# Two adjacent PSUM banks in one instruction: joined exponentials and joined row maxima in a two-attention kernel

## The chip, the cores and the metric

The kernel runs on one core of one Trainium2 chip. Its time is the device time of one execution in microseconds (us), and the figure that counts is the median of several runs. Five engines with queues of their own take part: TensorE (PE in the profile, with PEld for its weight loads), VectorE (DVE), ScalarE (ACT), GpSimd (POOL) and SyncE (SP, which here issues transfers). A matmul writes its result into PSUM, a memory of eight banks; one bank holds 512 float32 values in each of 128 partitions. ACT and DVE read the banks and so make them free again.

## The reference

Two attentions over the same 2048 tokens of width 576, mixed by a gate. A has a key and a value for each of its 32 heads; B has one key and one value that all its 32 heads share. A head has 18 columns.

```
x = A_x                                            # 1 x 2048 x 576
g = sigmoid((x * gate_w).sum(-1, keepdims=True))
# A: q, k, v of each head from x @ wqkv
p = softmax(einsum("bhqd,bhkd->bhqk", q, k) * 18 ** -0.5)
a = merge(einsum("bhqk,bhkd->bhqd", p, v)) @ wo
# B: q of each head from x @ wq; k = x @ wk, v = x @ wv for all heads
p = softmax(einsum("bhqd,bkd->bhqk", q, k) * 18 ** -0.5)
b = merge(einsum("bhqk,bkd->bhqd", p, v)) @ wo
out = g * a + (1 - g) * b
```

The B weights wq and wk are drawn eight times larger than the others, so its scores are large and each row's maximum has to be subtracted before the exponential.

## The kernel before

**The heads.** 64 heads are worked through one after the other, the 32 of B first. For one head there are 2048 x 2048 scores. They are needed twice: once to find each query row's maximum, and once, with the maximum already subtracted, for the exponential.

**A step.** A head has 16 steps, one for each tile of 128 rows. T counts steps from the first head to the last (1024 in all), and the loop at the end of the program advances by two steps, so that a head is eight *pairs* of steps. In a pair, with the tiles called A and B, there is:

- *Scores* (`step_scores`, L553): four matmuls a tile (`sA0` to `sB3`), each of 128 keys against 512 queries into one PSUM bank `ps`; after each an exponential on ACT (L560) from the bank into `pt` in SBUF. Eight of each in a pair.
- *Maxima* (`step_max`, L515): matmuls of 128 queries against 512 keys into a bank `pm` (`mA2` and the like), for a head that is 22 steps (`LEAD`) ahead, and a row maximum on DVE (L524) of each. Of the first tile of a pair, two of the four pieces are taken together: a matmul `x` with the difference of two pieces of keys goes into a `ps` bank, ACT writes its positive part to `xb` (L518), and DVE adds `xb` to the other piece and takes the maximum in one instruction (L521). So a pair has six plain maxima, one of L521, eight score matmuls, one `x`, and nine ACT instructions.
- *PV* (`step_pv`, L566): the exponentials times the values, accumulated over the whole head into one bank `acc`. Four matmuls for four groups of 512 queries stand side by side in four column groups of the array. A PV step can be done whole (512 columns) or in two halves (256). Scores and PV are one pair apart: the pair T does the PV of steps T-2 and T-1.

Score matmuls use partitions 0 to 55 and maxima partitions 64 to 117, so a score and a maximum that follow each other can run in the array at the same time; two scores, or two maxima, cannot.

**The order.** Nothing is scheduled automatically. Strings of tokens give the order within a pair: `s` and `m` as above, `x`, then `P`/`Q` for a whole PV step and `p`/`f`/`h`/`H` for halves, and `U` for a unit of the output projection. `PLAIN` and its variants (`END`, `AFTER`, `BEFORE_ROWS`, `ROWS`) are used where no unit is due. `UNIT` and `UNIT_END` are for 32 pairs between T = 522 and T = 848, where the projection of the B heads is spread out (heads with one unit and heads with two). `UNIT2` is for 25 pairs between T = 944 and T = 998, nearly every pair there. A unit (`out_proj`, L695) is 12 matmuls of 288 columns into a `pm` bank and one ACT or DVE instruction that adds it to `oacc`. The last 11 pairs have orders of their own (`ALONE`, `LAST`).

**Other work around it.** At the end of a head DVE copies `acc` to `oe` (`head_out`, L588), and three pairs before a head begins its maxima are reduced and transposed (`max_rows`, L530 and L532). SP carries the queries and keys of the next heads and the heads' outputs. About every seventh head DVE also computes reciprocals of row sums (L617).

**PSUM.** Three pools: `ps_s` with four banks (`ps`: scores, `x`), `ps_m` with three (`pm`: maxima, units) and `ps_o` with one (`acc`). A matmul waits until the bank that comes round in its pool has been read. `pt` has 12 slots of 512 values.

## Time and profile before

| | |
|---|---|
| median of 3 runs | 2668.65 us (2668.41 to 2670.15) |
| span of the profiled execution | 2669.7 us (no other time of that execution is recorded) |
| granted TensorE clock in it | 0.999 |
| PE busy | 2652.4 us (99%) |
| DVE busy | 2421.4 us (91%) |
| ACT busy | 2393.3 us (90%) |
| POOL busy | 283.8 us (11%) |

Stages, by the copies of `acc` to `oe` that end each head and by the first score matmul at 275.4 us: projections and set-up until about 275 us; 32 heads and a half without units until about 1437 us, of 35.5 to 36.1 us each; 22 heads with one or two units until about 2250 us, of 36.0 to 39.0 us; 5 heads without units until about 2393 us; then 7 units a head, 46.4 to 46.7 us each, and the last head and the end of the projection.

The profile's busy share of ACT and DVE counts an instruction from its start to its end; two that follow each other overlap a little, so the mean duration of one is longer than the distance between two. PE's matmuls are pipelined, so its busy share says little; its work is better read from the distances between starts, or from the chain of waits, where a piece ends when the next begins.

### The profile page before, as it was taken

What the parts mean: (1) busy time and instruction counts of PE and PEld (TensorE: products, weight loads), DVE (VectorE), ACT (ScalarE), POOL (GpSimd) and SP (SyncE); (2) the same over time, 40 slices, a digit from 0 to 9 for tenths busy, and PEclk for the clock granted to TensorE, in tenths of its full rate; (3) what the DMA queues carried; (4) which work ended last, traced back from release to release, by engine and by line L of the source; (5) the groups of instructions that cost most, each with busy time, mean ns of one, the idle gap of its engine ahead of it and who ended that gap; (6) DMA issues with size and microseconds to landing.
All of it is one profiled execution on the core that took longest, in us unless ns stands there. A gap on an engine that the chain in (4) does not pass through costs nothing.

```text
span 2669.7 us, 58607 instructions
## 1 busy us (share of the span) xinstructions
PE 2652.4 (99%) x22278; PEld 898.0 (34%) x22278; DVE 2421.4 (91%) x4588; ACT 2393.3 (90%) x4814; POOL 283.8 (11%) x526
## 2 busy tenths in 40 slices
PE   9999999999999999999999999999999999999998
PEld 7778322222222222222222222222222222223444
DVE  8447999999999999999999999999999999998873
ACT  4341899999999999999999999999999999998875
POOL 4740000001001100100110002000200011001000
PEclk9999999999999999999999999999999999999999
DMA  7332000011001100210132112112121212122312
GB/s 202 125 112 76 23 20 20 20 37 40 28 17 46 44 20 18 54 33 20 36 77 82 43 53 85 43 55 59 58 67 51 55 54 61 40 70 86 90 36 95
DMA packets 127304, 150.15 MB, mean 56 GB/s; under 512 B 55456, under 2 KB 94744, under 8 KB 125933
## 3 DMA queue, kind: packets, MB, share of 16 engines
q1 hardware_dynamic: 112593, 119.38, 15.7%
q0 software_dynamic: 8096, 19.30, 2.1%
q10 hardware_dynamic: 6332, 7.71, 0.8%
q8 instruction: 175, 2.87, 0.4%
q14 instruction: 108, 0.88, 0.1%
HBM read 90.80 MB, written 46.45 MB: 51 GB/s over the span
## 4 chain that ended last, share of the span: by engine, by line
PE 93%; DVE 5%; ACT 1%; DMA 1%; issue 1%; SPq 0%; ACTq 0%; DVEq 0%
PE acc L566 38%; PE ps L553 26%; PE pm L515 13%; PE pm L695 4%; PE ps L515 4%; PE ps L248 3%; PE pm L248 3%; DVE mx L524 2%; PE ps L297 2%; DVE junk L521 0%; ACT pt L560 0%; DVE norm_a L190 0%; DVE pl L262 0%; DMA R<-r_d 0%; DVE oacc L772 0%
## 5 line engine op out<-in xcount | busy, mean ns | idle before, releaser
L560 ACT ACTIVATE pt<-ps 128x512 f32<-128x512 f32 x4074 | 2105.6, 651 | 63.1 <-PE ps L553 51.5
L524 DVE TENSOR_REDUCE mx<-pm 128x1 f32<-128x512 f32 x3072 | 1914.1, 682 | 68.0 <-PE pm L515 34.0
L553 PE MATMUL ps<-qs,ksb 56*128 56x512 f16 x2688 | 807.3, 380 | 0.0
L515 PE MATMUL pm<-ksb,qs 54*128 54x512 f16 x2341 | 762.5, 380 | 1.1 <-DVE mx L524 0.6
L566 PE MATMUL acc<-pt,vb 128*19 128x256 f32 (+1 forms) x6144 | 592.4, 457 | 0.0
L566 PE MATMUL acc<-pt,vg 128*19 128x256 f32 (+1 forms) x5496 | 561.7, 480 | 0.3
L515 PEld LDWEIGHTS <-qs 54*128 54x128 f16 x4096 | 293.1, 94 | 516.1 <-issue 455.4
L553 PE MATMUL ps<-qs,ksa 56*128 56x512 f16 x1386 | 407.5, 380 | 0.3
L515 PE MATMUL pm<-ksa,qs 54*128 54x512 f16 x1232 | 399.8, 380 | 1.6 <-DVE mx L524 1.1
L553 PEld LDWEIGHTS <-ksb 56*128 56x128 f16 x2688 | 202.4, 93 | 487.5 <-issue 446.3
L521 DVE CUSTOM_DVE_ANT_0 junk<-pm,xb 128x512 bf16<-128x512 f32 x501 | 341.0, 681 | 9.4 <-PE pm L515 9.0
L518 ACT ACTIVATE xb<-ps 128x512 f32<-128x512 f32 x501 | 319.6, 638 | 7.7 <-PE ps L553 7.3
L534 POOL TENSOR_SCALAR mt<-mt 128x32 f32<-128x32 f32 x64 | 18.6, 290 | 1626.4 <-DVE mt L532 1626.4
L553 PEld LDWEIGHTS <-ksa 56*128 56x128 f16 x1408 | 100.6, 94 | 233.1 <-issue 213.5
L566 PEld LDWEIGHTS acc<-pt,vb 128*19 128x19 f32 x6144 | 104.3, 97 | 216.1 <-issue 208.6
L566 PEld LDWEIGHTS acc<-pt,vg 128*19 128x19 f32 x5496 | 93.2, 97 | 213.1 <-issue 209.7
L515 PE MATMUL ps<-kdb,qs 54*128 54x512 f16 x373 | 140.5, 377 | 0.1
L300 ACT ACTIVATE vst<-ps 128x288 f32<-128x288 f32 x32 | 13.2, 412 | 60.6 <-PE ps L297 60.6
L256 ACT ACTIVATE ph<-ps,tv 128x512 f16<-128x512 f32 x29 | 19.8, 687 | 49.3 <-PE ps L248 34.3
L256 ACT ACTIVATE ph<-pm,tv 128x512 f16<-128x512 f32 x27 | 18.3, 687 | 48.0 <-PE pm L248 29.4
L703 DVE TENSOR_TENSOR oacc<-pm,oacc 128x288 f32<-128x288 f32 x32 | 14.6, 457 | 46.0 <-PE pm L695 45.9
L262 DVE SCALAR_TENSOR_TENSOR pl<-pm,tv,ph 128x512 f16<-128x512 f32 x27 | 20.0, 748 | 37.5 <-ACT ph L256 24.5
(167 smaller groups left out, 1544.6 us busy)
## 6 DMA issues: line engine op xcount, KB each, us to landing
qs<-qkh SPq DMA_DIRECT2D x244, 72.0 KB
qs<-qkl SPq DMA_DIRECT2D x122, 72.0 KB
onh<-oh SPq DMA_DIRECT2D x32, 256.0 KB
onl<-ol SPq DMA_DIRECT2D x32, 256.0 KB
oih<-onh SPq DMA_DIRECT2D x16, 512.0 KB
oil<-onl SPq DMA_DIRECT2D x16, 512.0 KB
ot<-oe SPq DMA_DIRECT2D x220, 36.0 KB
qkh<-ph POOLq DMA_DIRECT2D x56, 128.0 KB, 2.1
```

The costliest lines, as they stand in the source:

```text
L248: nc.tensor.matmul(fp[:, a0:b0], w[a][:kr, k, :], X[b][:kr, k, s0 + a0:s0 + b0], start=(n == 0), stop=(n == len(PROJ) - 1), skip_group_che ...
L256: nc.scalar.activation(h, fp, AF.Copy, scale=t)
L262: nc.vector.scalar_tensor_tensor(l, fp, t, h, op0=OP.mult, op1=OP.subtract)
L297: nc.tensor.matmul(fp[:, 0:288], X[b][:kr, k, st_ * P:(st_ + 1) * P], w[a][:kr, k, :], start=(n == 0), stop=(n == len(PROJ) - 1))
L515: nc.tensor.matmul(pm, qs[u % 3][b:b + 54, i * P:(i + 1) * P], k, start=True, stop=True)
L518: nc.scalar.activation(MX["x", u, i], pm, AF.Relu)
L521: nc.vector.tensor_tensor_reduce(junk, pm, MX.pop(("x", u, i)), 1.0, -3e38, op0=OP.add, op1=OP.max, accum_out=MX[u][:, i, c:c + 1])
L524: nc.vector.tensor_reduce(MX[u][:, i, c:c + 1], pm, axis=AX.X, op=OP.max)
L553: nc.tensor.matmul(ps, kst(u)[b:b + 56, i * P:(i + 1) * P], qs[u % 3][b:b + 56, x * 512:(x + 1) * 512], start=True, stop=True)
L560: nc.scalar.activation(pt, ps, AF.Exp, scale=SCALE / LIFT ** 2)
L566: nc.tensor.matmul(acc[32 * j:32 * j + 19, a:b], v_of(u, i), PT[u, i, j][:, a:b], start=(i == 0 and a == 0), stop=(i == 15), skip_group_ch ...
L695: nc.tensor.matmul(fp[:, 0:288], o[b][:r, t, s2 * P:(s2 + 1) * P], w[a][:r, t, 288 * hf:288 * hf + 288], start=(n == 0), stop=(n == 3 * nt ...
```

## The change

PSUM becomes one tile `bk` of eight banks: 0 to 3 for scores and `x`, 4 to 6 for maxima and units, 7 for `acc`. Two counters give the next bank of each ring (`next_s`, `next_m`) and are set to zero at the start of each head. `pt` becomes one tile of 16 slots, with a counter of its own.

Where the new order has an `S`, its score and the one before lie in adjacent banks, and one ACT instruction takes both banks, 1024 values, into two adjacent slots of `pt`. Where it has an `N`, its maximum and the one before are taken by one DVE instruction, which writes two columns, if their banks are adjacent (a unit shifts the ring, so that in heads with units some are not joined). A head without units has 11 joined exponentials and 7 joined maxima. Over the kernel there are 688 joined exponentials and 373 joined maxima.

The orders of all pairs up to T = 1000 are new: eight strings for the eight pairs of a head, with `c` for the piece that L521 reads, and `p0h`, `p0f`, `p1h`, `p1f` for half or whole PV steps of the earlier and the later tile. The same eight strings with `U` at the end are used where a unit is due.

```diff
-    ps_s = ctx.enter_context(tc.tile_pool(name="ps_s", bufs=4, space=PSUM))
-    ps_m = ctx.enter_context(tc.tile_pool(name="ps_m", bufs=3, space=PSUM))
-    ps_o = ctx.enter_context(tc.tile_pool(name="ps_o", bufs=1, space=PSUM))
+    ps = ctx.enter_context(tc.tile_pool(name="ps", bufs=1, space=PSUM))
...
-    acc = ps_o.tile([P, 512], F32, name="acc")
+    bk = ps.tile([P, 8, 512], F32, name="bk")
+    acc = bk[:, 7, :]
+    RING = {"s": 0, "m": 0}
+
+    def next_s():
+        RING["s"] += 1
+        return (RING["s"] - 1) % 4
+
+    def next_m():
+        RING["m"] += 1
+        return 4 + (RING["m"] - 1) % 3
...
-        L["pt"] = ctx.enter_context(tc.tile_pool(name="ppool", bufs=12, side="left"))
+        L["pt"] = ctx.enter_context(tc.tile_pool(name="ppool", bufs=1, side="left")).tile([P, 16, 512], F32, name="pt")
...
+        elif join == "first":
+            MX["j"] = (n, 4 * i + c)
+        elif join == "second":
+            n0, c0 = MX.pop("j")
+            assert (n, 4 * i + c) == (n0 + 1, c0 + 1)
+            flat = MX[u].rearrange("p i c -> p (i c)")
+            nc.vector.tensor_reduce(flat[:, c0:c0 + 2], bk[:, n0:n0 + 2, :], axis=AX.X, op=OP.max)
...
+    def exps(q):
+
+        if len(q) == 2 and q[0][0] + 1 != q[1][0]:
+            exps(q[:1])
+            exps(q[1:])
+            return
+        n, k = q[0][0], len(q)
+        t = next_pt(k)
+        nc.scalar.activation(L["pt"][:, t[0]:t[0] + k, :], bk[:, n:n + k, :], AF.Exp, scale=SCALE / LIFT ** 2)
...
-    PLAIN = "mB1 mB3 sA0 sA1 mA3 sA2 P mB2 sA3 x sB0 mA2 sB1 mB0 h sB2 mA0 H sB3"
-    UNIT2 = "sA0 mA3 sA1 mB0 sA2 P sA3 mB1 sB0 mB2 sB1 x U mA2 sB2 mA0 sB3 Q mB3"
...
+    PLAIN = ("s c s m S s N p0h m s p0h m s s m x s m p1f",
+             "s s m S N s m p0f x m s c S p1h s m s m p1h",
+             "m s s m p0h x s m s s m p0h s m N S p1h c s p1h",
+             "s m s m x m s p0f s c m s S N s p1h m S p1h",
+             "s c m s m s x p0h m s m s p0h s m S N s p1f",
+             "s m s m S m s p0f m s m x s s N p1h c s p1h",
+             "m s x m s S N p0h c s p0h m s s m s s m p1f",
+             "s c m x s m S p0h s m p0h s m m s S s m p1f")
...
+        if T % 16 == 0:
+            RING["s"] = RING["m"] = 0
...
+            if op in "sS":
+                k = ns.index(n)
+                step_scores(*divmod(T + k // 4, 16), k % 4, hold=k < 7 and ops[ns[k + 1]] == "S")
```

Three places in the order of the instructions follow. In the rows, `ps`, `pm` and `acc` are the banks before, `bk` any bank of the changed kernel; `pt` are exponentials, `xb` the positive part, `mx` the maxima of a head, `qs`, `ksa`, `ksb`, `kda` queries and keys, and a number behind a name tells one copy of a tile from another.

On ACT, over some pairs of a head without units, before:

```order
L560 ACTIVATE pt<-ps 128x512 x8
L518 ACTIVATE xb<-ps 128x512
L560 ACTIVATE pt<-ps 128x512 x10
L518 ACTIVATE xb<-ps 128x512
L560 ACTIVATE pt<-ps 128x512 x7
```

and changed:

```order
L577 ACTIVATE pt<-bk 128x512 x3
L530 ACTIVATE xb<-bk 128x512
L577 ACTIVATE pt<-bk 128x512 x2
L577 ACTIVATE pt<-bk 128x1024
L577 ACTIVATE pt<-bk 128x512 x2
L577 ACTIVATE pt<-bk 128x1024
L577 ACTIVATE pt<-bk 128x512 x2
L530 ACTIVATE xb<-bk 128x512
```

The count of exponentials in a head is the same; eleven times two of them have become one instruction of 1024 values.

On DVE, after the copy of `acc` at the end of a head, before:

```order
L588 COPY oe<-acc 128x512
L524 TENSOR_REDUCE mx_1891<-pm 128x1 x2
L521 ISA junk,mx_1891<-pm,xb 128x512
L521 ISA mx_1891 128x1
L524 TENSOR_REDUCE mx_1891<-pm 128x1 x10
```

and changed:

```order
L625 COPY oe<-bk 128x512
L541 TENSOR_REDUCE mx_1826<-bk 128x2
L543 TENSOR_REDUCE mx_1826<-bk 128x1 x2
L533 ISA junk,mx_1826<-bk,xb 128x512
L533 ISA mx_1826 128x1
L543 TENSOR_REDUCE mx_1826<-bk 128x1 x6
L541 TENSOR_REDUCE mx_1826<-bk 128x2
```

L541 is the joined maximum with two columns; the second instruction named L533 (L521 before) only reads the result of the first.

On PE, around a unit between T = 944 and T = 998, before:

```order
L553 MATMUL ps<-qs_93,ksb 128x512
L515 LDWEIGHTS qs_94
L515 MATMUL ps<-kda,qs_94 128x512
L695 MATMUL pm<-woh,oih 128x288 x4
L695 MATMUL pm<-woh,oil 128x288 x4
L695 MATMUL pm<-wol,oih 128x288 x4
L515 LDWEIGHTS qs_94
L515 MATMUL pm<-ksa_2748,qs_94 128x512
```

and changed:

```order
L588 MATMUL bk<-qs_87,ksb 128x512
L527 LDWEIGHTS qs_88
L527 MATMUL bk<-ksa_2561,qs_88 128x512
L603 MATMUL bk<-pt,vg 19x512 x4
L732 MATMUL bk<-woh,oih 128x288 x4
L732 MATMUL bk<-woh,oil 128x288 x4
L732 MATMUL bk<-wol,oih 128x288 x4
L588 LDWEIGHTS ksb
L588 MATMUL bk<-qs_87,ksb 128x512
```

The unit stood between scores and maxima and now stands behind a whole PV step, at the end of the pair.

More of the change, by code (lines that the diff above doesn't have):

```diff
@@ L241, in bank @@
     def bank(odd=False):
-        return ps_m.tile([P, 512], F32, name="pm") if odd else ps_s.tile([P, 512], F32, name="ps")
+        return mid() if odd else other()
     def products(fp, w, s0, a0, b0, gen=None, at=()):
@@ L294, in project_v @@
     def project_v(st_, hf, w):
-        fp = ps_s.tile([P, 512], F32, name="ps")
+        fp = other()
         for n, (a, b, k, kr) in enumerate(PROJ):
@@ L513, in step_max @@
             k = kst(u)[b:b + 54, c * 512:(c + 1) * 512]
-        pm = other() if c == "x" or spare else ps_m.tile([P, 512], F32, name="pm")
+        n = next_s() if c == "x" or spare else next_m()
+        pm = bk[:, n, :]
         nc.tensor.matmul(pm, qs[u % 3][b:b + 54, i * P:(i + 1) * P], k, start=True, stop=True)
@@ L732, in last_half @@
         yield
[L733 removed]
+        pt = mid()[:, 0:256]
         for c in range(2):
@@ L753, in end_bank @@
         n[0] += 1
-        return ps_s.tile([P, 512], F32, name="ps") if n[0] % 7 < 4 else ps_m.tile([P, 512], F32, name="pm")
+        return other() if n[0] % 7 < 4 else mid()
     def last_units():
@@ L761, in last_units @@
             end = END_T[st_ // 8]
-            fp = end_bank() if n > 1 else ps_m.tile([P, 512], F32, name="pm")
+            fp = end_bank() if n > 1 else mid()
             for m, (a, b) in enumerate(PRODS):
@@ L859, in gated_mix_kernel @@
         units = sum(due(t, Tb, Tc, 32) for t in (T, T + 1) for _, _, _, Tb, Tc in SEG)
-        order = LEADS if T < 0 else FIRST if T == 0 else LAST if T > TL else ALONE if alone else (UNIT2 if T >= SEG[1][3] else UNIT_END if T % 16 == 0 else UNIT) if units else \
-            {0: END, 2: AFTER if T > 2 else PLAIN, 8: BEFORE_ROWS, 10: ROWS}.get(T % 16, PLAIN)
+        if 0 <= T <= TL and not alone:
+            steps_pair(T, M, FIRST if T == 0 else pair_order(T, units), units)
+            units = 0
+            order = ""
+        else:
+            order = LEADS if T < 0 else LAST if T > TL else ALONE
         for op in order.split():
```

92 lines of the change are left out of this document (68 added, 24 removed), and 7 rows, old and new, of the table UNIT2.

## The prediction

> **What bounds the kernel now.** I read the busy shares first, then the same shares by stage, then how closely the instructions of each engine follow one another, and last the chain of waits. The page's first row and three stretches, each from one copy of `acc` to a later one (columns: PE, weight loads, DVE, ACT, POOL, each with its count, then clock and transfers):
>
> ```profile
> PE 2652.4 (99%) x22278; PEld 898.0 (34%) x22278; DVE 2421.4 (91%) x4588; ACT 2393.3 (90%) x4814; POOL 283.8 (11%) x526
> ...
> 316.43:1420.06 1103.63, 1103.32 (x9922) 282.97 (x9920) 1092.62 (x2083) 1101.00 (x2233) 83.23 (x153) 1.00 0.12 33
> 1456.04:2211.77 755.73, 755.07 (x6522) 218.97 (x6520) 714.02 (x1345) 729.13 (x1470) 53.78 (x99) 1.00 0.20 56
> 2430.28:2569.89 139.61, 138.32 (x1046) 56.68 (x1044) 115.68 (x223) 112.80 (x216) 6.18 (x13) 1.00 0.24 71
> ```
>
> The first stretch has no projection units. Its heads are counted by the copies of `acc` (32, 21 and 4 copies, so 31, 20 and 3 heads in the three stretches):
>
> ```profile
> L588 DVE COPY oe<-acc x32: 680/681/691, 316.4 to 1420.1; 128x512 f32<-128x512 f32 x32
> L588 DVE COPY oe<-acc x21: 684/686/686, 1456.0 to 2211.8; 128x512 f32<-128x512 f32 x21
> L588 DVE COPY oe<-acc x4: 684/685/686, 2430.3 to 2569.9; 128x512 f32<-128x512 f32 x4
> ```
>
> So a head takes 35.60 us without units (35.53 in most; the heads with DVE's reciprocals take half a microsecond more), 37.79 with one or two, 46.54 with seven. In the first stretch ACT is busy for 1101.0 of 1103.6 us: it is the bound there. In the second it idles 26.6 us, in the third 26.8 of 139.6.
>
> Busy shares count waits inside an instruction, so I worked out what each engine needs for one head at its own pace. ACT and DVE, in order of time (start, duration):
>
> ```profile
> 600.40 4.14 ACT L560 ACTIVATE pt<-ps 128x512 f32<-128x512 f32 x8
> 604.37 0.66 ACT L518 ACTIVATE xb<-ps 128x512 f32<-128x512 f32 x1
> ...
> 600.02 1.28 DVE L524 TENSOR_REDUCE mx<-pm 128x1 f32<-128x512 f32 x2
> 601.22 0.68 DVE L588 COPY oe<-acc 128x512 f32<-128x512 f32 x1
> 601.82 1.28 DVE L524 TENSOR_REDUCE mx<-pm 128x1 f32<-128x512 f32 x2
> 603.01 0.68 DVE L521 CUSTOM_DVE_ANT_0 junk<-pm,xb 128x512 bf16<-128x512 f32 x1
> 603.62 0.08 DVE L521 DVE_READ_ACCUMULATOR2_ANT mx<- 128x1 f32 x1
> ```
>
> The eight exponentials end at 604.54 and the next ACT instruction at 605.03: 0.49 us apart when ACT has a queue. A head has 72 of them, 35.3 us. DVE's starts lie 0.60 us apart (two from 600.02 to 601.22, the copy to 601.82), 0.61 with the read-out of L521: 48 maxima, 8 of L521 and the copy make 28.8 + 4.9 + 0.6 = 34.3, and the two small ones of `max_rows` about 0.4: 34.7 us.
>
> PE, from the chain of waits (start, length of the piece), one half of a PV step, a single slot, and the start of a longer run, with one whole PV step ahead:
>
> ```profile
> 602.06 0.98 PE acc L566 x8
> ...
> 604.13 0.56 PE acc L566 x8
> 604.68 0.32 PE ps L553
> ...
> 605.01 0.56 PE acc L566 x8
> 605.57 0.32 PE ps L553
> ...
> 605.89 0.21 PE ps L553
> ```
>
> A slot is one score and one maximum side by side, or one of them alone. A run of slots between PV costs 0.32 + 0.215 for each further slot; whole PV 0.985, half 0.56. The old `PLAIN` has runs of 4, 4 and 1 slots (`sB3 mB1 | mB3 sA0 | sA1 mA3 | sA2`, and so on), one whole PV and two halves: 3 x 0.32 + 6 x 0.215 + 0.985 + 2 x 0.56 = 4.355 us, 34.85 a head. So three engines need 35.3, 34.85 and 34.7 us and the head takes 35.53: 0.25 us is lost between the first of them and the others.
>
> With seven units a head the chain holds nothing but PE over a whole pair, 2443.73 to 2449.53, with the unit as the piece of 1.79 us:
>
> ```profile
> 2443.73 0.32 PE ps L553
> ...
> 2444.49 1.79 PE pm L695 x12
> 2446.27 0.32 PE pm L515
> ...
> 2446.59 0.21 PE pm L515
> ...
> 2446.81 0.98 PE acc L566 x8
> 2447.80 0.32 PE pm L515
> ...
> 2448.12 0.21 PE pm L515
> ...
> 2448.33 0.21 PE pm L515
> ...
> 2448.55 0.98 PE acc L566 x8
> 2449.53 0.32 PE ps L553
> ```
>
> There PE alone is the bound: 8 slots in runs of 3, 2 and 3, two whole PV steps and a unit, 0.96 + 5 x 0.215 + 1.97 + 1.79 = 5.80.
>
> **The change, part by part.**
>
> *Joined exponentials.* No instruction of 1024 values from PSUM stands in the trace; the nearest rows are copies of ACT and subtractions of DVE from SBUF at both sizes:
>
> ```profile
> L136 ACT ACTIVATE wh<-wst 128x512 fp32r<-128x512 f32 x14 | 8.7, 624 | 3.9 <-DMA wst<-wall 3.9
> L339 ACT ACTIVATE xh<-xs 128x1024 fp32r<-128x1024 f32 x8 | 8.4, 1056 | 0.5 <-DMA xs<-xT 0.4
> ...
> L139 DVE TENSOR_TENSOR wl<-wst,wh 128x512 fp32r<-128x512 f32 x3 | 2.1, 692 | 5.0 <-ACT wh L136 4.9
> L341 DVE TENSOR_TENSOR xl<-xs,xh 128x1024 fp32r<-128x1024 f32 x8 | 9.8, 1221 | 1.2 <-ACT xh L339 1.1
> ```
>
> 512 more values cost ACT 0.432 us, so a joined one takes 0.49 + 0.432 = 0.922 in a queue instead of 0.98: 0.058 saved, 0.64 a head, ACT 34.65 us. That is the whole fixed part of 0.49 - 0.432, and the upper bound. The lower is a loss: if a joined one did not overlap its neighbours it would take its whole 1.056, 0.076 more than two, and ACT 36.1 us a head. But ACT's instructions overlap in the rows above (the last exponential ends at 604.54, its successor started at 604.37), whatever they hold, so I take the saving.
>
> *Joined maxima.* 512 more values cost DVE 0.529; 0.07 saved each, 0.5 a head: 34.2 us. DVE is not the bound, so by itself this brings nothing.
>
> *The new orders on PE, without units.* Seven of the eight pairs again have 9 slots in runs of 4, 4 and 1, one whole PV and two halves: 4.355. The third has 8 slots in 2, 3, 2 and 1 and four halves: 4 x 0.32 + 4 x 0.215 + 4 x 0.56 = 4.38. A head: 34.87. PE does not shrink, and is now the engine that needs most. So at best a head falls from 35.53 to 34.87, by 0.66; at worst, with what is lost between engines unbounded, by nothing. In between, I step to the loss that the trace shows: 0.25 us in these heads before; zero in the pair of the last chain, where ACT and DVE had ample room. ACT keeps only 0.2 us of room, so I take 0.25: 35.12, a gain of 0.41. There are 38.2 such heads (T = 0 to 520 and 850 to 942): -15.7 us. DVE's reciprocals cost 0.54 in six of them; with 0.5 more room I take a quarter of that: -1.5.
>
> *Heads with one or two units.* The unit pairs had two whole PV steps and now have one and two halves, as above, and 9 slots for 8: 6.145 after, against 5.80 (against 6.0 at a head's start, where the next pair then needs one slot more). By these counts PE needed 36.5 or 37.9 us, 37.2 on average, and took 37.79. It now needs 36.67 or 38.45, 37.57 on average. With 0.25 lost, 37.82: +0.03 each, 22 heads, +0.6. Bounds are no loss, -4.8, and the old 0.59, +8.
>
> *Seven units a head.* 5.80 becomes 6.145: one slot more and two halves for a whole PV step, both paid on the engine that is the bound, with the runs 4, 1 and 4 for 3, 2 and 3: +0.35 in each of 25 pairs, +8.75. Seven pairs at 5.80 and one at 4.355 make 44.95 of the measured 46.54, so 1.6 a head was lost at the seams; part of it may go: -1.5 (bounds 0 and -6).
>
> *PSUM as one tile, rings, 16 slots.* The matmuls wait for the same engine as before, one each, and those of the second bank of a joined pair often for none. Slots are never late: a PV step frees its slots one pair before the ring returns. I cost this at nothing; the cover is that one pair (4.4 us). Where the ring of maxima is set to zero, bank 4 comes back after one other bank; a whole PV step of 0.985 us lies ahead, in which DVE works off what waits. The queues of SP and POOL carry the same transfers in the same order. Set-up and tail keep their orders: nothing.
>
> Sum: -15.7 - 1.5 + 0.6 + 8.75 - 1.5 = -9.3 on the span of 2669.7. The median lies 1 us below that span, so I forecast 2668.65 - 9.3 = **2659 us**.
>
> **The rivals.**
>
> *A joined instruction holds two banks until it ends* (slower). A score that needs the first of them waits 0.43 us longer than before, two of four banks are out of use for 0.92 us, and PE, the new bound, has nothing else to run. The place is every `S` and `N` without units. For it speaks that heads with units, bound by PE and with 1.6 us and more of room on ACT, still lost 0.59 each; against it, that these had orders with long PV and unit stretches. At 0.59 everywhere: -0.07 x 38.2 + 0.37 x 21 + 8.75 = +14, 2682 us. It decides from about 0.37 lost per head on, where the gain without units equals the rest. The Trainium skill, PSUM — Partial Sum Buffer, section "PSUM bank collisions raise a hardware error", says that two engines may not touch one bank and quadrant at once and that banks are to be guarded whole; the waits of this kernel agree with it, and it speaks for this rival.
>
> *The fixed part is paid per bank.* Then ACT stays at 35.3, heads without units stay, units cost as above: about +9, 2677 (with the whole 1.056 some 20 us more). Against it stand the two ACT rows.
>
> *Nothing is lost any more*: every stage runs at PE's need: -25.2 - 1.5 - 4.8 + 8.75 - 4 = -26.8, 2642. For it speaks the last chain; against it that ACT and PE are then only 0.2 us apart.
>
> *PE has room* and the time follows ACT alone: 0.64 x 38.2 = -24.4, units cost nothing: 2644. The Trainium skill, Perfetto Trace Analysis, section "Identifying the Most-Contended Engine", would have PE's headroom judged by the weight loads' busy share and not by its matmuls'. In the first stretch that share is 283 of 1103.6 us, which would speak for this rival; the trace does not agree, since the chain of the seven-unit pairs has PE back to back with weight loads at 57 of 139.6 us.
>
> *The one tile makes matmuls wait for other banks.* A score then waits for the latest exponential, some 0.4 us a slot: far over 2700. The waits in the order are the old ones, so this is unlikely.
>
> **How the numbers follow.** Forecast 0.50, two banks held 0.20, nothing lost 0.15, fixed part per bank 0.06, PE has room 0.05, false waits 0.04. About 0.2% (5.3 us) is what a measurement of this kernel can tell from no change. Of the forecast's 0.50, whose loss per head may lie between 0.1 and 0.4, 0.31 falls below 2663.3, 0.17 within, 0.02 above; of the 0.20, 0.06 within; the fast cases give 0.20. Faster 0.51, same 0.25, slower 0.24. The range 2643 to 2682 reaches to the fast and to the slow rivals and leaves out little of each; the forecast's own is 2651 to 2667.
>
> **What would show it.** Right: heads without units at 35.0 to 35.25 us with ACT below 99% busy there; a joined exponential 0.43 longer than a single one; seven-unit pairs 6.1 us apart; one- and two-unit heads at 36.9 and 38.7. Wrong: a head without units above 35.3 with gaps on PE ahead of the scores that follow a joined instruction, or seven-unit pairs still at 5.8.

## The result and the profile after

The changed kernel takes 2687.48 us (median of 4 runs, 2686.46 to 2688.55); the kernel before, on the same chip, 2669.4. The ratio is 1.0067, 95% interval 1.0053 to 1.0081: slower by 0.67%, where 2659 us was forecast.

The profiled execution's span is 2686.6 us against 2669.7. The three stretches after, from one copy of `acc` to a later one as in the prediction (columns: PE, weight loads, DVE, ACT, POOL, each with its count, then clock and transfers), and the copies that count the heads (31, 20 and 3 heads between them):

```profile
322.44:1421.53 1099.09, 1097.25 (x10172) 305.90 (x10169) 1078.93 (x1865) 1095.95 (x1892) 83.12 (x153) 1.00 0.12 34
1458.66:2225.40 766.74, 760.60 (x6922) 247.22 (x6921) 702.38 (x1255) 721.89 (x1251) 53.65 (x99) 1.00 0.19 55
2440.04:2583.97 143.93, 143.90 (x1238) 62.99 (x1238) 114.14 (x211) 107.91 (x184) 6.14 (x13) 1.00 0.24 71
```

```profile
L625 DVE COPY oe<-bk x32: 677/680/682, 322.4 to 1421.5; 128x512 f32<-128x512 f32 x32
L625 DVE COPY oe<-bk x21: 677/679/681, 1458.7 to 2225.4; 128x512 f32<-128x512 f32 x21
L625 DVE COPY oe<-bk x4: 676/678/682, 2440.0 to 2584.0; 128x512 f32<-128x512 f32 x4
```

The stretches took 1103.63, 755.73 and 139.61 us before. So the first gained 4.5 us, and the other two lost 11.0 and 4.3. The first row's own start shows another loss: the copy that ends head 0 stands at 322.44 and not at 316.43. From these copies, the kernel divides as follows (a plain head has no projection units and no reciprocals):

| part | before, us | after, us | difference |
|---|---|---|---|
| set-up and head 0 | 316.4 | 322.4 | +6.0 |
| heads 1 to 31 (a plain one) | 1103.6 (35.53) | 1099.1 (35.36) | -4.5 |
| heads 32 to 53 | 830.0 | 841.0 | +11.0 |
| ... one unit / two units | 36.97 / 38.44 | 37.11 / 39.34 | +0.14 / +0.90 |
| heads 54 to 58 | 180.2 | 177.5 | -2.7 |
| heads 59 to 62 (seven units a head) | 182.5 | 188.9 | +6.4 |
| rest | 56.9 | 57.7 | +0.8 |

One piece of work changes its row here. In the kernel before, the unit of T = 944 ran ahead of the copy that ends head 58, and this head took 37.57 us; now ten of its twelve matmuls run behind that copy, and the head takes 35.36, like a plain one. These 2.0 us above a plain head of before are in the row of heads 54 to 58 before and in the next row after. With them taken off, the two differences are about -0.7 and +4.3.

The joined instructions, from the groups of the first stretch (count, busy time, mean of one in ns, idle time before them). The joined exponential is 429 ns longer than a single one and the joined maximum 540, as forecast from the set-up's rows (432 and 529):

```profile
L577 ACT ACTIVATE pt<-bk 128x512 f32<-128x512 f32 x1303 | 708.4, 612 | 0.5
L577 ACT ACTIVATE pt<-bk 128x1024 f32<-128x1024 f32 x341 | 354.9, 1041 | 2.7 <-PE bk L588 1.7
L543 DVE TENSOR_REDUCE mx<-bk 128x1 f32<-128x512 f32 x1055 | 657.1, 681 | 0.0
L541 DVE TENSOR_REDUCE mx<-bk 128x2 f32<-128x1024 f32 x217 | 264.9, 1221 | 0.0
```

So the instructions cost what was counted, and the heads without units still gained 0.17 us each and not 0.41. That, the units and the set-up are three separate questions.

### The profile page after: what moved, and what is told of

Same layout as the page of the kernel before. It is cut to its first block, busy times and chain, and to the rows that moved or that the text cites. A ratio compares the mean times of both kernels' runs of the same rounds, so it can differ in the third digit from the quotient of the medians.

```text
span 2686.6 us, 59787 instructions
## 1 busy us (share of the span) xinstructions
PE 2660.8 (99%) x23238; PEld 965.7 (36%) x23238; DVE 2389.8 (89%) x4215; ACT 2373.8 (88%) x4126; POOL 283.3 (11%) x526
## 3 DMA queue, kind: packets, MB, share of 16 engines
q1 hardware_dynamic: 112593, 119.38, 15.7%
## 4 chain that ended last, share of the span: by engine, by line
PE 81%; ACT 8%; DVE 7%; DMA 1%; issue 1%; SPq 0%; POOL 0%; ACTq 0%; DVEq 0%; POOLq 0%
PE bk L603 32%; PE bk L527 18%; PE bk L588 18%; ACT pt L577 7%; PE bk L259 6%; PE bk L732 4%; DVE mx L543 4%; PE bk L308 2%; DVE junk L533 2%; ACT xb L530 1%; DVE mx L541 1%; DMA xs<-xT 0%; SPq L56 0%; DMA wst<-wall 0%; PE bk L797 0%
## 5 line engine op out<-in xcount | busy, mean ns | idle before, releaser
L577 ACT ACTIVATE pt<-bk 128x512 f32<-128x512 f32 (+1 forms) x3408 | 2072.9, 698 | 66.1 <-PE bk L527 33.8
L543 DVE TENSOR_REDUCE mx<-bk 128x1 f32<-128x512 f32 x2348 | 1461.7, 681 | 73.2 <-PE bk L527 49.8
L588 PE MATMUL bk<-qs,ksb 56*128 56x512 f16 x2688 | 800.0, 381 | 2.2 <-ACT pt L577 1.7
L527 PE MATMUL bk<-ksb,qs 54*128 54x512 f16 x2363 | 749.5, 381 | 4.5 <-DVE mx L543 1.4
L603 PE MATMUL bk<-pt,vb 128*19 128x256 f32 (+1 forms) x6400 | 598.9, 446 | 0.3 <-PE bk L527 0.3
L603 PE MATMUL bk<-pt,vg 128*19 128x256 f32 (+1 forms) x6200 | 579.3, 445 | 0.0
L541 DVE TENSOR_REDUCE mx<-bk 128x2 f32<-128x1024 f32 x373 | 455.2, 1220 | 1.6 <-PE bk L527 1.5
L588 PE MATMUL bk<-qs,ksa 56*128 56x512 f16 x1408 | 406.4, 381 | 0.3
L527 PE MATMUL bk<-ksa,qs 54*128 54x512 f16 x1232 | 395.6, 380 | 4.3 <-DVE mx L533 0.5
L533 DVE CUSTOM_DVE_ANT_0 junk<-bk,xb 128x512 bf16<-128x512 f32 x501 | 342.8, 684 | 35.5 <-ACT pt L577 27.9
```

What stands on the lines that cost most here:

```text
L527: nc.tensor.matmul(pm, qs[u % 3][b:b + 54, i * P:(i + 1) * P], k, start=True, stop=True)
L533: nc.vector.tensor_tensor_reduce(junk, pm, MX.pop(("x", u, i)), 1.0, -3e38, op0=OP.add, op1=OP.max, accum_out=MX[u][:, i, c:c + 1])
L541: nc.vector.tensor_reduce(flat[:, c0:c0 + 2], bk[:, n0:n0 + 2, :], axis=AX.X, op=OP.max)
L543: nc.vector.tensor_reduce(MX[u][:, i, c:c + 1], pm, axis=AX.X, op=OP.max)
L577: nc.scalar.activation(L["pt"][:, t[0]:t[0] + k, :], bk[:, n:n + k, :], AF.Exp, scale=SCALE / LIFT ** 2)
L588: nc.tensor.matmul(bk[:, n, :], kst(u)[b:b + 56, i * P:(i + 1) * P], qs[u % 3][b:b + 56, x * 512:(x + 1) * 512], start=True, stop=True)
```

## The experiments

Unless another is named, each edit is made to the changed kernel. Head times are read from the copies of `acc`, as above, so one kernel can answer for several stretches. Ratios are to the kernel before, with their 95% intervals.

### Which part of the change: joins, unit orders, staging, the tile

**All joins undone, the new orders kept.**

```diff
-            exps(q)
+            for e in q:
+                exps([e])
...
-                  if ops[n] == "N" and at_bank[nm[k - 1]] + 1 == at_bank[n]}
+                  if False}
```

> The changed kernel with its new orders, its one PSUM tile and its 16 slots, but every exponential and every row maximum is an instruction of its own again. Theory A (a joined instruction holds two banks, and PE waits for them): heads with two units, where ACT and DVE have over 3 us of room without joins, fall from 39.34 us to about 38.7, and heads with one from 37.11 to about 36.9. Theory B (the loss lies in the orders: where units and whole PV steps follow each other ACT and DVE run dry, and PE then waits for them): heads with units stay within 0.15 us of 39.34 and 37.11. Heads without units: ACT needs 35.3 us again, so both say 35.4 to 35.8; below 35.35 neither. Time: A about 2690, B about 2697.

Measured: 2700.98 us, ratio 1.0113 (1.0083 to 1.0142). Plain heads 35.54, with one unit 37.30, with two 39.50; heads 32 to 53 together 844.9. The joins are worth some 0.18 us in every one of these heads; they harm nowhere. That PE loses time because a joined instruction holds two banks is refuted, and the loss in heads 32 to 62 lies in what remains: the orders, the rings and the slots.

**The unit pairs with their orders of before.** Old strings, single instructions, in the 57 pairs that hold a unit.

```diff
+        if 0 < T <= TL and not alone and units:
+            if T % 16 == 0:
+                RING["s"] = RING["m"] = 0
+            order = UNIT2_OLD if T >= SEG[1][3] else UNIT_END_OLD if T % 16 == 0 else UNIT_OLD
-        if 0 <= T <= TL and not alone:
+        elif 0 <= T <= TL and not alone:
```

> The changed kernel, but the 57 pairs with a projection unit take their old orders (two whole PV steps, the unit between scores), without joins in those pairs; all other pairs stay new, with their joins. Theory B: heads with one or two units come back to 36.9 to 37.1 and 38.4 to 38.6, heads with seven units to 46.5, and the time to about 2672. Theory A: the joins in the other seven or six pairs still hold banks, and a head with two units stays above 39.0, since only two of its eight pairs change; heads with seven units come back all the same; time about 2681.

Measured: 2677.55 us, ratio 1.0027 (1.0016 to 1.0038). Heads 59 to 61 fall from 47.98 to 46.06 (46.5 before), heads with one unit to 36.80. Heads with two stay at 39.23. So the unit orders are the whole loss in the last heads and not the loss of the two-unit heads.

**The staging pool allocated first.** The 16 exponential slots lie where the set-up's staging tiles lay.

```diff
+    stp = ph1.enter_context(tc.tile_pool(name="stp", bufs=3, side="right"))
     xpool = ph1.enter_context(tc.tile_pool(name="xpool", bufs=1, side="right"))
     wpool = ph1.enter_context(tc.tile_pool(name="wpool", bufs=2, side="right"))
-    stp = ph1.enter_context(tc.tile_pool(name="stp", bufs=3, side="right"))
```

> The changed kernel, but the pool of the staging tiles is allocated ahead of the others, at the far end of SBUF, so that the tile of 16 slots no longer lies on memory from which stores still read. Theory C (the first exponential waits for the last stores, since all 16 slots are one tile): the first exponential follows its score by 0.4 us instead of 2.6, the first head ends about 2.4 us earlier against the first score than in the changed kernel, time about 2685. Rival (the TensorE clock, 0.83 in that stretch, or the first order itself): no difference, 2687.5.

Measured: 2686.86 us, ratio 1.0057 (1.0034 to 1.0080), span 2682.8; head 0 ends at 318.77 and not at 322.44. Of these 3.7 us, 0.8 lie ahead of the first score (278.18 against 278.95) and 2.9 behind it. The medians differ by only 0.6 us, less than the runs of either kernel do, so the effect is read from the traces. In order of time, ACT's first exponentials in the changed kernel, and then with the pool moved:

```profile
278.93 0.33 ACTq L56 DMA_DIRECT2D v_d<-vst  x1
...
281.55 3.04 ACT L577 ACTIVATE pt<-bk 128x512 f32<-128x512 f32 x6 [2.65 <-DMA v_d<-vst]
282.20 0.58 PE L588 MATMUL bk<-qs,ksb 56*128 56x512 f16 x1 [1.69 <-ACT pt L577]
```

```profile
278.16 0.33 ACTq L56 DMA_DIRECT2D v_d<-vst  x1
278.65 4.03 ACT L577 ACTIVATE pt<-bk 128x512 f32<-128x512 f32 x8 [0.52 <-PE bk L527]
```

The slots are one tile now, so the first exponential waits until every staging tile that lay under any slot has been stored: 2.65 us behind a store that had only just been issued. PE stands still for 1.69 us of it, and its granted clock is at half for 6.8 us from then on. The eleven microseconds from the first score in the kernel before, in the changed one, and in the mended one below (the last but two is the granted clock):

```profile
275.38:286.43 11.05, 10.63 (x67) 2.85 (x70) 9.39 (x19) 9.57 (x20) 0.00 (x0) 0.85 0.05 18
```

```profile
278.95:290.00 11.05, 8.92 (x44) 1.89 (x43) 6.75 (x11) 7.17 (x14) 0.00 (x0) 0.69 0.05 18
```

```profile
274.64:285.69 11.05, 10.25 (x75) 2.96 (x74) 9.79 (x18) 10.48 (x20) 0.00 (x0) 1.00 0.06 18
```

44 matmuls against 67 and 75 in the same time. The drop is not the stop's alone: the kernel before spent 3.4 us at half clock here, with no stop of PE over 0.2 us, and so did the changed kernel with the pool moved. What the kernels with the stop have in common is a longer drop: 6.8 us in each of the six whose engines do all their work.

**PSUM as three tiles of four, three and one bank**, to see whether the one tile adds waits.

```diff
-    bk = ps.tile([P, 8, 512], F32, name="bk")
-    acc = bk[:, 7, :]
+    bs = ps.tile([P, 4, 512], F32, name="bs")
+    bm = ps.tile([P, 3, 512], F32, name="bm")
+    acc = ps.tile([P, 512], F32, name="acc")
```

> The changed kernel, but PSUM is three tiles (four banks, three banks, one bank) instead of one; rings, joins and orders stay. Theory D (with one tile an instruction that reads a bank waits for matmuls into other banks): the evictions of the projection stage no longer wait 1.5 to 3 us each, the last product ends about 2.8 us earlier, and the instruction that takes xb no longer waits for exponentials (27 us in all); time about 2683 to 2685. Rival (the rings, not the tile): all as in the changed kernel, 2687.5.

Measured: 7218 us, ratio 2.70 (2.69 to 2.71). Groups of this kernel:

```profile
L583 ACT ACTIVATE pt<-bs 128x512 f32<-128x512 f32 x3386 | 2314.5, 684 | 3408.5 <-PE bs L594 2247.3 <-PE bm L533 1152.7 <-PE bm L594 5.9
L594 PE MATMUL bs<-qs,ksb 56*128 56x512 f16 x2688 | 1499.0, 586 | 780.2 <-ACT pt L583 618.9 <-ACT xb L536 147.5 <-DMA ksa<-ones_r 0.5
```

Neither expected outcome came. Scores wait for exponentials of other banks of the same tile and the other way round, as the prediction's last rival had it for the one tile, which shows nothing of the kind. So this run says nothing on the one tile, only that a tile of several banks can be tracked as a whole. Why the tile of eight banks escapes that stays open.

**The one tile alone**, put to the question from the other side: the kernel before, its three PSUM pools replaced by rings over one tile, and nothing else.

```diff
-    ps_s = ctx.enter_context(tc.tile_pool(name="ps_s", bufs=4, space=PSUM))
-    ps_m = ctx.enter_context(tc.tile_pool(name="ps_m", bufs=3, space=PSUM))
-    ps_o = ctx.enter_context(tc.tile_pool(name="ps_o", bufs=1, space=PSUM))
+    bk = ctx.enter_context(tc.tile_pool(name="ps", bufs=1, space=PSUM)).tile([P, 8, 512], F32, name="bk")
+    class Ring:
+        def __init__(self, first, n):
+            self.first, self.n, self.at = first, n, 0
+        def tile(self, shape, dtype, name=None):
+            self.at += 1
+            return bk[:, self.first + (self.at - 1) % self.n, :]
+    ps_s, ps_m, ps_o = Ring(0, 4), Ring(4, 3), Ring(7, 1)
```

> The kernel before with one edit: its PSUM pools of four, three and one bank become one tile of eight banks, handed out by the same rings; orders, twelve exponential slots and single instructions stay. Theory E (the one tile costs only in the set-up, where an eviction waits until the next job's products are through): first scores near 278.2 us instead of 275.4, first exponential within 1 us of it, plain heads 35.5, heads with one projection unit 37.0, with two 38.4, heads with seven 46.5; time near 2672. Theory F (the shared tile also adds waits among scores, maxima and units): heads with two units 39.2 as in the two runs that have the one tile, heads with seven above 47, time 2680 or more.

Measured: 2673.46 us, ratio 1.0012 (1.0003 to 1.0021). Plain heads 35.55, with one unit 36.99, with two 38.47, heads 59 to 61 46.5: the kernel before, to 0.03 us in heads with up to two units. First scores at 277.71 and not at 275.38. So the tile and its rings cost next to nothing among the heads, and about 2.3 us in the set-up. By the end of head 0, 1.3 of these are left (317.71 against 316.43): from the first score on this kernel, whose clock does not drop there, takes 40.0 us and the kernel before 41.1.

Where these arise is seen around the seventh projection job, the one after the transposition at 30 us. The kernel before, then the changed one (start, duration, and in brackets the idle time before with its releaser):

```profile
29.30 0.42 PE L284 MATMUL ps<-ident,pst 18*128 18x18 f32 x4
...
30.39 1.20 PE L248 MATMUL ps<-xh,wh 128*128 128x512 f32 x4 [0.67 <-ACT xh L339]
...
32.54 1.41 DVE L262 SCALAR_TENSOR_TENSOR pl<-ps,tv,ph 128x512 f16<-128x512 f32 x2
```

```profile
30.05 0.42 PE L295 MATMUL bk<-ident,pst 18*128 18x18 f32 x4
...
33.30 1.41 DVE L273 SCALAR_TENSOR_TENSOR pl<-bk,tv,ph 128x512 f16<-128x512 f32 x2
...
34.11 2.08 PE L259 MATMUL bk<-xh,wh 128*128 128x512 f32 x4 [3.64 <-DVE pl L273]
```

Before, the job started at 30.39, so the pool had given it a bank that was free by then, while the second and third job's banks were still read at 32.54. The ring goes by turns: after the three first jobs (banks 0 to 2), the mask's transposition (3) and the next transposition (0), it gives bank 1, the second job's, and PE waits 3.64 us. Then it runs at half its clock: the four matmuls after those shown take 1.91 us against 1.09. The granted clock from that matmul on, after and before:

```profile
34.11:39.40 5.29, 5.29 (x13) 4.13 (x14) 4.07 (x7) 3.26 (x6) 4.66 (x9) 0.50 0.57 192
```

```profile
34.20:39.00 4.80, 4.80 (x23) 3.89 (x22) 4.01 (x7) 3.62 (x6) 4.43 (x9) 1.00 0.67 226
```

The Trainium skill, TensorE: Matmul & The Clock Gate, section "HAM oscillation — how this bites in real kernels", states that PE's idle gaps must stay under some 3.4 us or the clock falls to half; the drop beside 3.64 us of idleness here agrees with it. As a bound it does not hold here: this stop lasted from 30.47 to 34.11, and the clock was at half from 32.72 on, 2.25 us into it; at the first exponential it fell beside a stop of 1.69 us, and in the kernel before beside none over 0.2.

### Units and the ring's reset

**Old orders in all pairs of heads 32 to 53 and in the pairs of heads 59 to 62**; with it the staging pool first, and a job's eviction issued ahead of the next job's products (`flush()` moved up by one line in `project`).

```diff
+        if 0 < T <= TL and not alone and (units or 512 <= T < 864):
+            if T % 16 == 0:
+                RING["s"] = RING["m"] = 0
+            order = (UNIT2_OLD if T >= SEG[1][3] else UNIT_END_OLD if T % 16 == 0 else UNIT_OLD) if units else \
+                {0: END_OLD, 2: AFTER_OLD, 8: BEFORE_ROWS_OLD, 10: ROWS_OLD}.get(T % 16, PLAIN_OLD)
```

> The changed kernel with three edits, in three separate stretches: every pair of heads 32 to 53 and every pair with a unit has its order of before (no joins there); the staging pool is allocated first; a set-up job's eviction is issued ahead of the next job's products. Theory B (orders): heads with one unit 37.0, with two 38.45, heads 32 to 53 together 830, heads with seven 46.1, plain heads before 32 and after 53 35.36. Theory E for the set-up: first scores back at 275.4 to 276, head 0 ends near 316.5. Together about 2660, under the kernel before. If the sixteen slots or the one tile make the second unit dear, two-unit heads stay at 39.2 and the time is 2667 or more; if the set-up's late start has another cause, first scores stay at 278 and it is 2663.

Measured: 2672.93 us, ratio 1.0010 (1.0001 to 1.0019). One-unit heads 37.00, two-unit heads 38.85: 0.4 us too many even with the orders of before, now once in each such head. First scores stay at 279.0, so the early eviction was not the point.

The 0.4 us stands at the end of a two-unit head. In this kernel, and then in the kernel before, the last maximum of the head (L533, L521) and the score and maximum that follow:

```profile
1527.11 0.68 DVE L533 CUSTOM_DVE_ANT_0 junk<-bk,xb 128x512 bf16<-128x512 f32 x1
1527.32 0.39 PE L588 MATMUL bk<-qs,ksb 56*128 56x512 f16 x1
1527.71 0.09 DVE L533 DVE_READ_ACCUMULATOR2_ANT mx<- 128x1 f32 x1
1527.85 0.37 PE L527 MATMUL bk<-ksa,qs 54*128 54x512 f16 x1
```

```profile
1527.64 0.68 DVE L521 CUSTOM_DVE_ANT_0 junk<-pm,xb 128x512 bf16<-128x512 f32 x1
1527.84 0.39 PE L553 MATMUL ps<-qs,ksb 56*128 56x512 f16 x1
1527.84 0.39 PE L515 MATMUL pm<-ksa,qs 54*128 54x512 f16 x1
```

Before, score and maximum start together. With the ring, the maximum starts 0.53 us later, when DVE is through with the one before: a head has 56 maxima in the ring of three, and two units make 58, so the last one lies in the ring's first bank, and the reset at the next head's start hands out that bank again.

**No reset in heads 32 to 53**, all orders and joins of the changed kernel kept; in the set-up, the mask's transposition takes bank 3 without moving the ring.

```diff
-        if T % 16 == 0:
+        if T % 16 == 0 and not 512 <= T < 864:
             RING["s"] = RING["m"] = 0
...
     def turn_mask():
-        pt = other()
+        pt = bk[:, 3, :]
```

> The changed kernel with all its orders and joins; the bank rings are not reset at the starts of heads 32 to 53, and the mask transposition leaves the ring where it is. Theory G: first scores at 275.4 to 276.5 us; two-unit heads (39.34) lose the wait behind a bank just filled, 0.2 to 0.4, and keep the rest of their 0.9, which is then the orders': 38.95 to 39.15; one-unit heads may lose joins that no longer lie side by side (up to 0.18): 37.1 to 37.3. If the reset is all of it: two-unit heads 38.45.

Measured: 2680.84 us, ratio 1.0043 (1.0028 to 1.0058). Two-unit heads 38.86, so the reset is 0.48 of their 0.90 us, a little more than expected, and the orders the rest; one-unit heads 37.10. First scores at 276.29, 2.7 us earlier. (They scatter between kernels whose set-up is the same: 277.3 to 279.0 us in the six measured so far with bank 1 for that job.)

**The three mendings together**: the bank in the set-up, the staging pool first, and in heads 32 to 53 no reset and the old orders in two-unit heads; all pairs with a unit, those of heads 59 to 62 too, have their old orders.

```diff
+        if 0 < T <= TL and not alone and (units or 512 <= T < 864 and T // 16 % 2 == 0):
+            if T % 16 == 0 and T >= 864:
+                RING["s"] = RING["m"] = 0
...
```

> The changed kernel with edits in three separate stretches. Set-up: the small mask transposition takes bank 3 without moving the ring on, so that the seventh projection job gets bank 0 (its copies are done by 28.9 us) and not bank 1 (33.5 us). First exponential: the staging pool is allocated first. Heads 32 to 53: heads with two units have their orders of before, heads with one unit only in the unit's pair, and the bank rings are not reset at the start of these heads; the pairs of the heads with seven units have their old order. Theory G (the ring hands out the wrong bank in the set-up; the reset hands out the bank just filled): first scores at 275.4 to 276.5 us, two-unit heads 38.45, one-unit heads 36.8 to 37.0, the rest as in the earlier run with old orders from head 32 on; span 2664 to 2666, just under the kernel before. If the set-up waits for something else: first scores 278 and span 2667. If the reset isn't it: two-unit heads stay at 38.85.

Measured: 2663.06 us, ratio 0.9974 (0.9965 to 0.9984): faster than both kernels. First scores at 274.64, head 0 ends at 315.13, two-unit heads 38.44, one-unit heads 36.80, heads 32 to 53 together 828.4. Two-unit heads have the same orders as in the run with old orders and the reset, 38.85, so there the reset alone cost 0.41. The seventh job's matmul waits for its operand again, as before the change:

```profile
30.95 1.20 PE L259 MATMUL bk<-xh,wh 128*128 128x512 f32 x4 [0.69 <-ACT xh L350]
```

### Why the joins brought so little

**Only the exponentials joined**, and **only the maxima joined**: one of the first experiment's two edits at a time.

> The changed kernel with its joined maxima split into single ones; the joined exponentials stay. Plain heads were 35.36 with both kinds of joins and 35.54 with none. If the exponentials bring the 0.18 us: 35.36, one-unit heads 37.1, time near 2688. If the maxima bring it: 35.54, and time near 2700. If each brings half: 35.45.

> The changed kernel with its joined exponentials split into single ones, issued where the joined one was; the joined maxima stay. If the exponentials bring the 0.18 us of a plain head: 35.54 or more and time near 2700; if the maxima bring it: 35.36 and time near 2688. Each half: 35.45.

Measured: 2692.70 us, ratio 1.0083 (1.0065 to 1.0101), and 2695.22, ratio 1.0092 (1.0074 to 1.0111). Plain heads 35.49 with joined exponentials and 35.41 with joined maxima, between 35.54 and 35.36. The exponentials, which the forecast's main gain was to come from, bring 0.05 us; the maxima, which were to bring nothing, 0.13.

**Engines made light one after the other.** Exponentials and maxima on a quarter of the columns (in the first of the three kernels the rectified copies too), then each alone.

```diff
-        nc.scalar.activation(L["pt"][:, t[0]:t[0] + k, :], bk[:, n:n + k, :], AF.Exp, ...)
+        nc.scalar.activation(L["pt"][:, t[0]:t[0] + k, 0:128], bk[:, n:n + k, 0:128], AF.Exp, ...)
...
-            nc.vector.tensor_reduce(MX[u][:, i, c:c + 1], pm, axis=AX.X, op=OP.max)
+            nc.vector.tensor_reduce(MX[u][:, i, c:c + 1], pm[:, 0:128], axis=AX.X, op=OP.max)
```

> The changed kernel with exponentials, maxima and rectified copies on the first 128 of the 512 columns of a bank only; the other columns of the exponentials are 1.0 throughout. This leaves work of ScalarE and VectorE out and all of TensorE's in. Theory H (TensorE's own need is 34.87 us a plain head as summed, and the 0.49 above it in the changed kernel is waiting at hand-overs): plain heads 34.8 to 35.0, one-unit heads 36.7, two-unit heads 38.4. Theory I (TensorE needs more than the sum, which is why the joins brought so little): plain heads 35.25 to 35.4, one-unit heads 37.0, two-unit heads 38.9 or more.

> The changed kernel with its exponentials on the first 128 of the 512 columns of a bank only, the other columns being 1.0; maxima and rectified copies are whole. It leaves most of ScalarE's work out and all of VectorE's and TensorE's in. Plain heads were 35.36 with all work and 34.89 with both engines light. If the 0.47 us between is waiting for ScalarE, whose exponentials stand at 34.65 us a head in the sum: 34.9 to 35.0. If it is waiting for VectorE (34.2 in the sum): 35.3. If each engine alone still costs a part: between.

> The changed kernel with its maxima on the first 128 of the 512 columns of a bank only, exponentials whole; it leaves most of VectorE's work out and all of ScalarE's and TensorE's in. Plain heads: 35.36 with all work, 35.29 with light exponentials, 34.89 with both light. If VectorE alone holds the 0.47 us: 34.9 to 35.0. If TensorE and ScalarE lose time between them as the prediction had it (0.25 on top of the larger): 35.1 to 35.15. If ScalarE's own need is above its sum of 34.65: more than 35.2.

Measured, plain heads: 34.89 us with both light, 35.29 with light exponentials, 35.07 with light maxima. The 31 heads of the first stretch, by kernel in this order:

```profile
326.90:1408.60 1081.70, 1081.70 (x10170) 270.42 (x10172) 480.77 (x1864) 493.19 (x1891) 83.04 (x153) 1.00 0.13 34
```

```profile
330.77:1427.90 1097.13, 1095.27 (x10172) 287.47 (x10170) 1077.05 (x1866) 565.88 (x1891) 83.12 (x153) 1.00 0.13 34
```

```profile
322.10:1409.50 1087.40, 1087.40 (x10170) 297.51 (x10169) 482.57 (x1864) 1086.44 (x1892) 83.21 (x153) 1.00 0.13 34
```

With ACT's work halved, DVE's is unchanged (1077.05 after 1078.93 us) and so, nearly, is the time; with DVE's work light it falls by 0.29 us a head. So DVE is what the changed heads mostly wait for. With DVE light, ACT and PE lose 0.18 us between them over PE's 34.89, somewhat less than the 0.25 of the forecast. (In the first two of these kernels the columns left out are set once, ahead of head 0; the stretches start behind that.)

What holds DVE, beside its own work, is above all a wait ahead of the maximum that takes in the rectified copy (L521, now L533). Its group in the first stretch, before, after, and with light exponentials:

```profile
L521 DVE CUSTOM_DVE_ANT_0 junk<-pm,xb 128x512 bf16<-128x512 f32 x248 | 168.7, 680 | 4.8 <-PE pm L515 4.8
```

```profile
L533 DVE CUSTOM_DVE_ANT_0 junk<-bk,xb 128x512 bf16<-128x512 f32 x248 | 169.8, 685 | 15.8 <-ACT pt L577 11.0 <-PE bk L527 1.2
```

```profile
L534 DVE CUSTOM_DVE_ANT_0 junk<-bk,xb 128x512 bf16<-128x512 f32 x248 | 170.0, 685 | 15.8 <-PE bk L528 11.8 <-ACT pt L578 0.3
```

It idles 15.8 us where it idled 4.8, while the other maxima, quoted above, idle 0.0. One such place of the changed kernel, in order of time:

```profile
599.29 2.47 DVE L543 TENSOR_REDUCE mx<-bk 128x1 f32<-128x512 f32 x4
...
600.32 1.05 PE L603 MATMUL bk<-pt,vb 128*19 128x512 f32 x8
601.31 0.39 PE L588 MATMUL bk<-qs,ksb 56*128 56x512 f16 x1
601.31 0.39 PE L527 MATMUL bk<-ksb,qs 54*128 54x512 f16 x1
...
601.88 0.69 DVE L533 CUSTOM_DVE_ANT_0 junk<-bk,xb 128x512 bf16<-128x512 f32 x1
```

The four maxima start (2.47 - 0.68) / 3 = 0.597 us apart, so the next could start at 601.68; it starts at 601.88, since its matmul stands behind a whole PV step on PE. Four of the eight pairs of a plain head have such a wait, of 0.26, 0.06, 0.29 and 0.20 us by the same reckoning (the 0.06 behind a half PV step): 0.81 a head. No run moves this matmul, so the place is read from the trace and not shown by an experiment. The name ACT in the group after is the last event of several; with ACT light the same wait is put down to PE.

## Why the prediction was wrong

It had the sign wrong, and the time lies outside its range. Step by step:

- **Joined exponentials, 0.43 us longer than single ones:** right (0.429), and "fixed part per bank" is out. "Heads without units at 35.0 to 35.25" is wrong (35.36), and so is ACT below 99% busy there: 1095.95 of 1099.09 us, since its instructions contain their waits.
- **PE's needs of 34.87, 36.67 and 38.45 us:** right: with light engines these heads take 34.89, 36.68 and 38.46.
- **ACT needs 35.3 us and is the bound, so 0.25 is lost, before and after:** this is the step that failed for the plain heads. The 0.49 us was read between two ends. Of the 2231 distances between ACT's starts in the first stretch before, 1422 are 0.476 to 0.480 us and none is shorter, which makes 34.4 a head. So PE's 34.85 was the largest need already, the head stood 0.68 above it, and joined exponentials could take nothing from it. After the change 0.47 are left above PE's 34.89, so that the gain was 0.17 and not 0.41.
- **"DVE is not the bound, so by itself this brings nothing", at 34.7 us before and 34.2 after:** this failed with it; light engines show that most of the 0.47 is waiting for DVE. Counted by its starts, a head after the change needs 34 x 0.598 + 7 x 1.14 + 8 x 0.617 + 0.598 for the copy + 0.575 for the two small ones = 34.43, and 0.81 in front of L533 makes 35.24 of the 35.36 measured. The sum took an engine's own pace for its need and left out its waits. By the same count the old orders need 34.81 and took 35.53, so DVE waited 0.72 us a head in them too, more than the profile's idle time shows (4.8 + 1.8 us for 31 heads), since an idle gap counts only what exceeds the usual overlap of 0.08. Joining took 0.39 off DVE's need, and 0.2 of it came back as waits. That DVE held the kernel before as well follows from this count; no run with light engines was made of that kernel.
- **The two sums that rest on these steps:** the -15.7 us came to about -5 (heads 1 to 31 -4.5, heads 54 to 58 -0.7 without the unit that changed its row). The reciprocals' -1.5 did not come: these heads, five and not six, take 36.09 as before (36.08).
- **Loss of 0.25 between ACT and PE alone:** 0.18 where DVE is out of the way. The size was nearly right for these two; the third engine was missing.
- **Heads with one or two units, 36.9 and 38.7, together +0.6 (bounds -4.8 and +8):** they took 37.11 and 39.34, together +11.0. The step that failed is "Where the ring of maxima is set to zero, bank 4 comes back after one other bank": behind two units it comes back at once, 0.48 us a head, and without the reset heads 32 to 53 are 4.4 us shorter, within the bounds again. What remains above PE's need, 38.86 against 38.46 and 37.11 against 36.68, is again a loss of 0.4 where 0.25 was taken.
- **Seven units, 5.80 to 6.145 us a pair, +8.75 - 1.5 = +7.25:** the place and the price of a pair are right: two units of such pairs start 6.13 us apart (2439.76 and 2445.89), and with light engines these heads take 47.56, with all work 47.98, so PE is nearly alone there, as the quoted chain had it. The sum is +4.3, without the unit that changed its row, and within its bounds: the seams gave back about 4.4 us and not 1.5.
- **"PSUM as one tile, rings, 16 slots ... I cost this at nothing", and "Set-up and tail keep their orders: nothing":** +6.0 us by the end of head 0, 3.6 of them ahead of the first score and 2.4 behind it. The waits counted were those among the heads, where the cost is indeed nothing. In the set-up the ring gives out banks by turns where the pool had given a free one, and the slots as one tile wait for all memory under them; behind both stalls PE runs at half clock for some microseconds.
- **The rivals.** Two banks held: the time, 2682, is near, the mechanism is not. One tile and false waits among the heads: not so here, but that is what three tiles did. Nothing lost, and PE having room: out, with 35.36 against 34.87 and PE back to back where units are dense. (By the shares named, the chances of the same time and of a slower one add to 0.23 and 0.26, not 0.25 and 0.24.)

Part by part, forecast and measured: plain heads -17.2 and -5.2, heads with one or two units +0.6 and +11.0, seven units +7.25 and +4.3, set-up and head 0 nothing and +6.0, the tail nothing and +0.8. That is -9.3 forecast and +16.9 measured on the span. What makes the tail 0.8 us longer stays open.

## What to carry to other kernels

Where three engines need nearly the same time, a sum of instructions by their own pace does not say which is the bound; make one engine's work light at a time and read the head's length, and look for the one instruction in front of which a busy engine waits, by the distances between starts rather than by the idle time. When pools become rings kept by hand, follow each ring through the places where the pattern is broken (the set-up, the extra unit, the reset) and ask which bank comes next and who still reads it; when many buffers become one tile, ask what its first writer must wait for. An edit with no cost in the loop may still pay in the set-up, where a stall of 2 to 4 us on PE or ACT also stood beside a lower PE clock.

## What the runs showed of the hardware that was not expected

After 3.64 us without a matmul PE ran at a granted clock of 0.50 for the next 5.29 us; the clock had fallen 2.25 us into the stop. Around a stop of 1.69 us among the first scores it was 0.69 on average over eleven, but 0.85 in the kernel before, which had no such stop, and 1.00 in the mended kernel, so what sets off that drop stays open. A wait of 2.65 us on ACT at the first exponential, with that drop, went with an end of head 0 that lay 3.7 us later (322.44 against 318.77 without it), 2.9 of them counted from the first score. A maximum over two banks takes 1221 ns and its successor starts 1.14 us after it, 0.06 less than two single ones at 0.598; over the seven of a head that is 0.39 us, of which 0.13 reached the head's length.
